# Last chunk of a fused attention and max-out kernel: first-half output products two blocks sooner, second-half token blocks completed one behind the other

## The chip, the cores and the metric

The kernel runs on one core of a Trainium2 chip (trn2). The metric is the device time of one execution in microseconds (us); the profile's span, from the first to the last instruction, is some 2 us shorter. Engines are called PE (TensorE), VectorE (DVE in the profile), ScalarE (ACT), GpSimd (POOL) and SP.

## The reference, cut to what matters

```python
def reference(q, k, v, tau, w1, w2, w3, w_out):       # q, k, v: (4, 6144, 256)
    ...                                               # attention over channels, gives x (24576, 256)
    h = np.maximum(np.maximum(x @ w1, x @ w2), x @ w3)   # (24576, 768)
    return h @ w_out                                     # (24576, 256), float32
```

The attention matrix is multiplied into the three weights ahead, so that for each chunk of 512 tokens the kernel computes three products per block of 128 hidden columns, takes their maximum, and multiplies by w_out. Only the last of 48 chunks is changed.

## The kernel before

The tokens of the last chunk go in two halves of two token blocks (256 columns). `h_block` makes one block of 128 of the 768 hidden columns (fc is 0 to 5): six matmuls on PE, one ScalarE copy, two VectorE maxima, and, where `two_copies` is set, a second ScalarE copy that gives the second maximum two bf16 operands outside PSUM, where the matmuls leave their results (the tiles h_ps and o_ps). The result of a block is called ht; a *product* below is one matmul of ht with w_out. PEld in the views is PE loading the weights of a matmul, here ht itself for a product.

```python
def h_block(gi, aw, fc, tsl=slice(0, TPC), two_copies=False):
    ...
    hp = []
    for m in range(3):
        t = htile(f"h_ps{m}")[:, :n]
        for ic in range(CC):
            PE.matmul(...)                                              # L432
        hp.append(t)
    s_mx = mx_pool.tile([P, CHUNK], BF16, name="s_mx")[:, :n]
    ACT.activation(out=s_mx, in_=hp[0], func=AF.Copy)                   # L436
    DVE.tensor_tensor(out=s_mx, in0=hp[1], in1=s_mx, op=ALU.max)        # L437
    last = hp[2]
    if two_copies:
        last = mx_pool.tile([P, CHUNK], BF16, name="s_h2")[:, :n]
        ACT.activation(out=last, in_=hp[2], func=AF.Copy)               # L441
    DVE.tensor_tensor(out=ht, in0=last, in1=s_mx, op=ALU.max)           # L442

def last_chunk(gi, aw, pending):
    ...
    def products(ps, t0, i, fcs): ...                                   # L504: one matmul for each fc

    def first_half(i):
        if i == 0:
            first["ps"] = xtile("o_ps")
        products(first["ps"], 0, i, range(FC))
        if i == HT - 1:
            ACT.activation(out=o_sb[:, 0:HT, :]..., in_=first["ps"], func=AF.Copy)   # L515
            SP.dma_start(out=dst[:, 0:HT, :], in_=o_sb[:, 0:HT, :])                  # L516

    for fc in range(FC):
        h_block(gi, aw, fc, slice(0, HT))                # first half; the chunk before is finished here too
        ...
    for fc in range(FC):
        h_block(gi, aw, fc, slice(HT, TPC), two_copies=fc in (0, 2, 3))
        if fc >= FC - HT:
            first_half(fc - (FC - HT))
    pss = [htile("o_ps") for _ in range(HT)]
    for fcs in (range(FC - 1), (FC - 1,)):
        for i in range(HT):
            products(pss[i], HT, i, fcs)
    ACT.activation(out=o_sb[:, HT, :], in_=pss[0][:, 0:d_model], func=AF.Copy)       # L531
    DVE.tensor_copy(out=o_sb[:, HT + 1, :], in_=pss[1][:, 0:d_model])                # L532
    ACT.dma_start(out=dst[:, HT, :], in_=o_sb[:, HT, :])                             # L533
    SP.dma_start(out=dst[:, HT + 1, :], in_=o_sb[:, HT + 1, :])                      # L534
...
keep_order(tc)       # every engine executes in the order in which the program is written
```

Because of `keep_order` each engine works in program order, and so an operation that has to wait holds up all that stand behind it on its engine.

## Time and profile before

| | before |
|---|---|
| time, median (lowest to highest) of the first 3 runs | 572.99 us (572.92 to 573.05) |
| span of the profiled run | 571.0 us |
| busy share PE / VectorE / ScalarE | 97% / 74% / 55% |
| granted PE clock | 1.0 |

The views are read from the end backwards: which engine did the last thing, what released it, and what each engine did in the microseconds ahead of that. The lines stand in the prediction, with how each is read. A bracket at the end of a line of a timeline is the idle time of that engine ahead of it, with what ended it; gaps up to 0.15 us get no bracket.

### The profile page before, as it was taken

How to read it: one execution, taken by the hardware profiler on the slowest of the kernel's cores; microseconds unless marked ns; L12 is line 12 of the kernel's file. 1: busy time of each engine (PE TensorE's matmuls, PEld its weight loads, DVE VectorE, ACT ScalarE, POOL GpSimd, SP SyncE). 2: the span in 40 equal slices, each digit the busy share in tenths (PEclk: the TensorE clock that was granted, in tenths of full speed). 3: DMA queues.
4: the chain of work that ended last, by engine and by line, in shares of the span. 5: the costliest groups of instructions: out<-in, count | busy, mean ns of one | idle time of the engine just before them, and what ended most of it. 6: DMA issues, size and time to landing. Idle time of an engine off the chain costs nothing.

```text
span 571.0 us, 9570 instructions
## 1 busy us (share of the span) xinstructions
PE 553.7 (97%) x3395; PEld 328.5 (58%) x3398; DVE 422.9 (74%) x663; ACT 316.4 (55%) x552; POOL 233.4 (41%) x237
## 2 busy tenths in 40 slices
PE   3799999999999999999999999999999999999997
PEld 2665555555755555555575555555575555555566
DVE  0378777877887777777767777777768778778775
ACT  1274567677464576776535467767635444444444
POOL 2442257776450078776560048776750000000000
PEclk9999999999999999999999999999999999999999
DMA  9995999894379169884179359894437333132111
GB/s 144 105 171 111 137 227 132 160 135 115 99 91 178 55 120 155 128 154 100 57 132 151 100 73 144 148 142 100 119 83 157 75 77 108 56 102 65 56 57 74
DMA packets 76960, 65.64 MB, mean 115 GB/s; under 512 B 52464, under 2 KB 62576, under 8 KB 76784
## 3 DMA queue, kind: packets, MB, share of 16 engines
q0 software_dynamic: 19072, 26.48, 38.8%
q1 hardware_dynamic: 57696, 38.41, 24.4%
q8 instruction: 26, 0.43, 0.3%
q14 instruction: 22, 0.18, 0.1%
q10 hardware_dynamic: 144, 0.13, 0.1%
HBM read 78.64 MB, written 25.17 MB: 182 GB/s over the span
## 4 chain that ended last, share of the span: by engine, by line
PE 93%; DMA 5%; POOL 0%; issue 0%; DVE 0%; ACT 0%; ACTq 0%; DVEq 0%; POOLq 0%
PE h_ps L432 65%; PE o_ps L479 22%; DMA q_sb<-in_q_dram 5%; PE gram L285 3%; PE ew_ps L331 3%; POOL k_sb L100 0%; PE o_ps L504 0%; PE h_ps L453 0%; PE ew_ps L359 0%; PE vt_ps L416 0%; DVE aw_sb L368 0%; PE warm_ps L201 0%; DVE o_sb L532 0%; ACT sqa L185 0%; PE rs_ps L353 0%
## 5 line engine op out<-in xcount | busy, mean ns | idle before, releaser
L432 PE MATMUL h_ps<-vt_sb,aw_sb 128*128 128x512 bf16 (+1 forms) x1758 | 404.9, 375 | 0.0
L432 PEld LDWEIGHTS <-aw_sb 128*128 128x128 bf16 x1758 | 171.3, 98 | 160.6 <-DVE aw_sb L337 2.4
L437 DVE TENSOR_TENSOR s_mx<-h_ps,s_mx 128x512 bf16<-128x512 f32 (+1 forms) x293 | 198.2, 676 | 79.2 <-ACT s_mx L436 78.9
L436 ACT ACTIVATE s_mx<-h_ps 128x512 bf16<-128x512 f32 (+1 forms) x293 | 171.7, 586 | 122.5 <-PE h_ps L432 121.2
L442 DVE TENSOR_TENSOR ht_sb<-h_ps,s_mx 128x512 bf16<-128x512 f32 (+1 forms) x290 | 198.3, 684 | 32.7 <-PE h_ps L432 1.9
L244 POOL TENSOR_TENSOR acc<-acc,sq 128x768 f32<-128x768 f32 x88 | 144.3, 1649 | 69.2 <-ACT sq L236 53.1
L479 PE MATMUL o_ps<-wo_sb,ht_sb 128*128 128x256 bf16 x1128 | 153.9, 273 | 0.0
L479 PEld LDWEIGHTS <-ht_sb 128*128 128x128 bf16 x1128 | 110.4, 98 | 52.2 <-DVE ht_sb L442 0.2
L482 ACT ACTIVATE o_sb<-o_ps 128x512 f32<-128x512 f32 x94 | 56.1, 597 | 83.9 <-PE o_ps L479 83.9
L111 POOL DMA_DIRECT2D v_sb<-in_v_dram x48 | 27.7, 582 | 38.7 <-DMA vt_sb<-v_sb 35.2
L236 ACT ACTIVATE sq<-q_sb 128x768 bf16<-128x768 fp8e4 x48 | 40.5, 845 | 0.0
L236 ACT ACTIVATE sq<-k_sb 128x768 bf16<-128x768 fp8e4 x48 | 40.1, 835 | 0.0
L241 POOL CAST acc<-sq 128x768 f32<-128x768 bf16 x6 | 4.9, 820 | 65.4 <-ACT sq L236 65.4
L103 POOL DMA_DIRECT2D q_sb<-in_q_dram x33 | 18.4, 565 | 3.5 <-DMA v_sb<-in_v_dram 3.1
L171 PE MATMUL kk<-k_sb 128*128 128x256 fp8e4 x48 | 7.5, 338 | 11.7 <-DVE k_sb L157 6.2
L100 POOL DMA_DIRECT2D k_sb<-in_k_dram x29 | 16.0, 554 | 3.0 <-DMA v_sb<-in_v_dram 1.1
L185 ACT ACTIVATE sqa<-q_sb 128x1024 bf16<-128x1024 fp8e4 (+2 forms) x9 | 6.8, 768 | 18.1 <-DMA q_sb<-in_q_dram 18.1
L285 PE MATMUL gram<-k_sb,q_sb 128*128 128x512 fp8e4 x144 | 16.8, 276 | 0.0
L334 ACT ACTIVATE aw_sb<-ew_ps,rinv 128x384 bf16<-128x384 f32 (+1 forms) x24 | 13.2, 554 | 5.7 <-PE ew_ps L331 4.8
L285 PEld LDWEIGHTS <-q_sb 128*128 128x256 fp8e4 x144 | 15.9, 136 | 0.6
L257 POOL PARTITION_ALL_REDUCE tot<-acc x6 | 10.9, 1858 | 12.1 <-DVE s_mx L437 6.1
L331 PE MATMUL ew_ps<-w_sb,et 128*128 128x384 bf16 (+1 forms) x96 | 15.8, 313 | 0.0
(73 smaller groups left out, 128.1 us busy)
## 6 DMA issues: line engine op xcount, KB each, us to landing
out_dram<-o_sb SPq DMA_DIRECT2D x41, 512.0 KB, 2.9
v_sb<-in_v_dram POOLq DMA_DIRECT2D x48, 256.0 KB, 4.3
k_sb<-in_k_dram POOLq DMA_DIRECT2D x24, 192.0 KB, 5.9
q_sb<-in_q_dram POOLq DMA_DIRECT2D x24, 192.0 KB, 7.3
out_dram<-o_sb SPq DMA_DIRECT2D x13, 256.0 KB, 2.0
k_sb<-in_k_dram POOLq DMA_DIRECT2D x5, 256.0 KB, 10.6
w_sb<-in_moe_w_dram POOLq DMA_DIRECT2D x9, 128.0 KB, 5.7
kf<-in_k_dram SPq DMA_DIRECT2D x1, 1024.0 KB, 4.7
```

Of the source, the lines that this page charges most:

```text
L103: POOL.dma_start(out=qk[b][0][:, g0:g0 + w, :], in_=q_r[b][:, g0:g0 + w, :])
L111: POOL.dma_start(out=t, in_=v_r[gi // NCH, gi % NCH])
L236: ACT.activation(out=sq, in_=src, func=AF.Square)
L244: POOL.tensor_tensor(out=acc, in0=acc, in1=sq, op=ALU.add)
L285: PE.matmul(g[:, j * C:(j + 1) * C], lhsT=qt[:, tsl, j * P:(j + 1) * P], rhs=kt[:, tsl, :], start=(tp == 0 and j == 0), stop=(tp == NG // ...
L331: PE.matmul(ew[:, :w], lhsT=et[:, j, ic * P:(ic + 1) * P], rhs=w_sb[m][:, j, fsl], start=(j == 0), stop=(j == CC - 1))
L432: PE.matmul(t.rearrange("p (t n) -> p t n", n=P), lhsT=aw[m][:, ic, fsl], rhs=vt[:, tsl, ic, :], start=(ic == 0), stop=(ic == CC - 1))
L436: ACT.activation(out=s_mx, in_=hp[0], func=AF.Copy)
L437: DVE.tensor_tensor(out=s_mx, in0=hp[1], in1=s_mx, op=ALU.max)
L442: DVE.tensor_tensor(out=ht, in0=last, in1=s_mx, op=ALU.max)
L479: PE.matmul(st["ps"][:, half], lhsT=ht[:, fc, t * P:(t + 1) * P], rhs=wo_sb[:, fc, :], start=(fc == 0), stop=(fc == FC - 1))
L482: ACT.activation(out=st["o"][:, t - 1:t + 1, :].rearrange("p t d -> p (t d)"), in_=st["ps"], func=AF.Copy)
```

## The change

Its intent, as far as the code tells it: do the output products of the first half (F0 and F1) after the second half's blocks 2 and 3 instead of 4 and 5, so that their output is copied and stored sooner; complete token block 0 of the second half ahead of block 1, so that its copy and store lie ahead of the other's and not beside it; and give the second ScalarE copy to other blocks.

```diff
--- before.py
+++ after.py
@@ -521,13 +521,13 @@
                 pending[fc - 1]()
         for fc in range(FC):
 
-            h_block(gi, aw, fc, slice(HT, TPC), two_copies=fc in (0, 2, 3))
-            if fc >= FC - HT:
-                first_half(fc - (FC - HT))
+            h_block(gi, aw, fc, slice(HT, TPC), two_copies=fc in (0, 1, 4))
+            if HT <= fc < 2 * HT:
+                first_half(fc - HT)
         pss = [htile("o_ps") for _ in range(HT)]
-        for fcs in (range(FC - 1), (FC - 1,)):
-            for i in range(HT):
-                products(pss[i], HT, i, fcs)
+
+        for i, fcs in ((0, range(FC - 1)), (1, range(2)), (0, (FC - 1,)), (1, range(2, FC))):
+            products(pss[i], HT, i, fcs)
         ACT.activation(out=o_sb[:, HT, :], in_=pss[0][:, 0:d_model], func=AF.Copy)
         DVE.tensor_copy(out=o_sb[:, HT + 1, :], in_=pss[1][:, 0:d_model])
         ACT.dma_start(out=dst[:, HT, :], in_=o_sb[:, HT, :])
```

## The prediction

> **What bounds the kernel now.** I read four views, in this order: the chain that ended last, in order of time; the timelines of PE, VectorE and ScalarE for the last chunk; and the DMA view of the last 5 us. The page says that PE is 97% busy over a span of 571.0 us at full clock, so only the last 12 us, which the change touches, matter here. I call the second-half blocks of the last chunk s0 to s5 (fc 0 to 5), and the two groups of six products of the first half F0 and F1.
>
> The chain, its last pieces (start us, us, what):
>
> ```profile
> 559.91 4.14 PE h_ps L432 x36
> 564.04 0.66 PE o_ps L504 x6
> 564.70 0.66 PE h_ps L432 x6
> 565.36 1.98 PE o_ps L504 x18
> 567.33 0.02 issue
> 567.36 0.42 DVE o_sb L532
> ```
>
> PE sets the end. Six matmuls of 256 columns take 0.66 us (0.109 each) in each of the short pieces. The 36 in the first piece should take 36 x 0.109 = 3.93 and take 4.14: PE waits some 0.2 us there, for PSUM buffers that VectorE has not yet read. The 36 are the last first-half block and s0 to s4; then come F0, s5, F1 and the twelve products of the second half. Behind PE stand the VectorE copy of the last token block (0.42), its store and the closing of the program.
>
> VectorE in the same stretch (start us, us, ...; the bracket is idle time before it):
>
> ```profile
> 560.85 0.42 DVE L437 TENSOR_TENSOR s_mx<-h_ps,s_mx 128x256 bf16<-128x256 f32 x1 [0.63 <-ACT s_mx L436]
> ...
> 564.04 0.42 DVE L437 TENSOR_TENSOR s_mx<-h_ps,s_mx 128x256 bf16<-128x256 f32 x1
> 564.56 0.29 DVE L442 TENSOR_TENSOR ht_sb<-s_h,s_mx 128x256 bf16<-128x256 bf16 x1
> 564.77 0.42 DVE L437 TENSOR_TENSOR s_mx<-h_ps,s_mx 128x256 bf16<-128x256 f32 x1
> 565.29 0.43 DVE L442 TENSOR_TENSOR ht_sb<-h_ps,s_mx 128x256 bf16<-128x256 f32 x1
> 565.63 0.41 DVE L437 TENSOR_TENSOR s_mx<-h_ps,s_mx 128x256 bf16<-128x256 f32 x1
> 566.15 0.43 DVE L442 TENSOR_TENSOR ht_sb<-h_ps,s_mx 128x256 bf16<-128x256 f32 x1
> ```
>
> From 560.85 to 566.58 VectorE has no bracket at all: it is the full engine of the tail, and works off the blocks about 0.6 us behind PE. From start to start: L437 to its L442 0.52; L442 to the next L437 0.34 if it reads PSUM, 0.21 if it reads ScalarE's copy ("two copies"). A block costs 0.86, or 0.73 with two copies, against 0.66 on PE. The last block's result (ht of s5) is there at 566.58; PE asks for it at about 566.83, after F1 and ten products. So there is 0.2 us to spare, and PE, not the latency of s5, sets the end.
>
> ScalarE, with F1's copy to o_sb last but one:
>
> ```profile
> 563.33 0.38 ACT L441 ACTIVATE s_h<-h_ps 128x256 bf16<-128x256 f32 x1
> 563.61 0.38 ACT L436 ACTIVATE s_mx<-h_ps 128x256 bf16<-128x256 f32 x1
> 564.95 0.38 ACT L436 ACTIVATE s_mx<-h_ps 128x256 bf16<-128x256 f32 x1 [0.96 <-PE h_ps L432]
> 566.10 0.60 ACT L515 ACTIVATE o_sb<-o_ps 128x512 f32<-128x512 f32 x1 [0.76 <-PE o_ps L504]
> 567.25 0.38 ACT L531 ACTIVATE o_sb<-o_ps 128x256 f32<-128x256 f32 x1 [0.56 <-PE o_ps L504]
> ```
>
> L515 runs after all six blocks' copies, where it holds up nothing. Back to back, 256-column copies start 0.28 apart (563.33, 563.61); after a 512-column copy the next starts 0.49 later (559.95 to 560.44 in the same timeline). A copy starts 0.31 after the start of the last matmul that it needs (s5: matmul 564.64, copy 564.95).
>
> The stores, 566 to 571 us in 40 slices of 0.125 us, and their landing:
>
> ```profile
> DMA  0000000000004999960029999940200000000000
> out_dram<-o_sb ACTq DMA_DIRECT2D x1, 128.0 KB, 1.9
> out_dram<-o_sb SPq DMA_DIRECT2D x1, 128.0 KB, 2.3
> ```
>
> The store of the first half moves in the first group of nines; the last two, issued 0.15 us apart (567.66 and 567.81 in the timelines), fill the second without a gap. The one issued second takes 2.3 us against 1.9. The span ends 0.9 us after that landing (570.1).
>
> **What the Trainium skill says.** "TensorE: Matmul & The Clock Gate", Part 2, step-by-step: PE pulls weight loads ahead, but matmuls stay in program order. The trace agrees: with a load one matmul ahead, matmuls follow each other every 0.109 us. So a product that waits for ht holds up all products behind it. "VectorE: DVE Perf Modes", the perf-mode tier table: tensor_tensor runs at 2x on 16-bit SBUF operands and 1x with any PSUM operand. The trace agrees in direction, 0.29 against 0.42. "DMA: Bandwidth & Descriptors", Anatomy of one DMA, gives a constant of about 2 us, mostly the write receipt (for the GpSimd path); these SP and ACT stores land after 1.9 to 2.3, of which the strip shows only about 0.45 us of movement for each of the last two. "PSUM — Partial Sum Buffer" bears on the flags of two interleaved groups, but they lie in two banks as before, so nothing follows for time.
>
> **The change part by part.** No instruction is added or removed, on any engine: 12 matmuls move ahead of s3 and s4, the order of the last 12 changes, and three blocks still have two copies, now 0, 1, 4. Everything is in orders and waits.
>
> PE up to s2 is as before; s2's last matmul starts at 562.26. Then, at 0.109 each: F0 562.37, s3 563.02, F1 563.67, s4 564.33, s5 564.98, products from 565.64. The two waits for PSUM in s3 and s4 (0.2 us) go, because F0 gives VectorE time. But s5 begins 0.45 later than before (564.98 against 564.54), since two groups of products (1.31 us) now lie ahead of it instead of one (0.66), less the 0.2.
>
> Between s5 and the first use of its ht only seven products remain (five of token block 0, two of block 1): 7 x 0.109 = 0.76, so PE asks for ht at 566.40. Before, sixteen lay between.
>
> When is it ready? F1's last matmul starts at 564.22, so L515 starts at 564.53 and stands in ScalarE's order ahead of the copies of s4. The first of these would be ready at 564.75 but starts at 564.53 + 0.49 = 565.02 and ends 565.40. Then VectorE: s3 is done at 564.98 (same sums of 0.86 and 0.73, other order), it idles to 565.43; s4 L437 565.43, L442 565.95, s5 L437 + 0.21 = 566.16, L442 + 0.52 = 566.68, end 567.11. (ScalarE's others: s4's second copy 565.30, s5's 565.58 to 565.96, both in time.) The load of the waiting product starts 0.05 after VectorE's end (555.64 to 555.69 at line 479 shows that), its matmul 0.11 later: 567.27. Four products of block 1 follow, the last at 567.27 + 4 x 0.109 = 567.70. Before it was 567.05 (567.36 less 0.31). So PE idles some 0.75 us, and the last VectorE copy is 0.65 later, at 568.01.
>
> In return block 0's copy is at 567.27 + 0.31 = 567.58, its store at about 568.0, block 1's store at 568.01 + 0.45 = 568.46. They are 0.46 apart instead of 0.15, about one movement's length, so the last should land after 2.0 instead of 2.3 us. That is 0.3 back.
>
> Sum: +0.65 on the chain, -0.3 on the landing = +0.35. 572.99 + 0.35 = 573.3.
>
> **The rivals.**
> 1. The order works as meant: s5's ht comes in time, PE loses no time, 0.2 of PSUM waits and 0.3 of store are won: 572.5. Against it: even with an idle ScalarE and VectorE, s5 from 564.98 needs 0.11 + 0.31 (second matmul, latency) + 0.41 (copy, hand-over) + 0.52 + 0.43 + 0.05 + 0.11 = 1.94, so the eighth product is at 566.92 and not at 566.51 and the last matmul at 567.36, 0.3 later than before. With the store's 0.3 that is a draw: 573.0. I count that draw as the real second case: it needs L515 not to delay s4.
> 2. The stores gain nothing: what made the second slower was the queue, not the other store. Then +0.65: 573.6. For it: only one pair is to be seen. Against it: the strip shows the two movements adjoining.
> 3. PSUM buffers go to blocks in another order and s5 waits for one of s4's (565.4). PE loses up to 0.3 there, but it is waiting later anyway; only if s5's first product got it would ht be 0.15 later: 573.5.
>
> **Range and chances.** The draw at 573.0 and the no-gain at 573.6 are on either side of 573.3; repeats agree to 0.13 us (572.92 to 573.05), and a changed program may shift stores by 0.1 to 0.2. So 572.7 to 573.8. Two per cent is 11.5 us, as much as the whole tail: within 2% is all but certain (0.99), faster 0.005, slower 0.005.
>
> **What would show it.** In the changed profile: L515 near 564.5 with s4's copy right behind it; a bracket of about 0.45 on VectorE before s4's L437; a wait of about 0.7 on PE's loads for ht in the last products; the chain passing from PE over VectorE's L442 and ScalarE instead of PE alone; the PSUM waits of s3 and s4 gone; the last two stores about 0.45 apart and the last landing near 2.0 us. I am wrong if PE runs through the products without a wait, if the time is below 572.7, or if the last store still takes 2.3.

## The result

| | before | changed |
|---|---|---|
| median of 4 runs (lowest to highest) | 572.95 us (572.67 to 573.05) | 573.16 us (573.11 to 573.44) |
| ratio | | 1.0005, 95% interval 0.9988 to 1.0023 |
| span of the profiled run | 571.0 us | 571.4 us |

A ratio is the mean time of one kernel's fast runs over that of the other's of the same rounds, so it is not quite the ratio of the two medians. The four runs of each do not overlap, but the interval includes 1: a time within 2% is certain. The medians are 0.21 us apart, less than the 0.33 to 0.38 us over which the runs of one kernel spread, so that the changed kernel is slower at all is suggested and not shown by the times alone. The traces show more, because they can be compared part by part.

For that a common zero is needed. The whole changed run lies 0.07 us later already in front of the changed part: VectorE's first operation with a bracket in the last chunk starts at 560.92 and not at 560.85. So 0.07 is taken off all times of the changed kernel below where the text says "aligned".

The chain that ended last, in order of time, of the changed kernel (start us, us, what):

```profile
559.98 2.62 PE h_ps L432 x24
562.60 0.66 PE o_ps L504 x6
563.25 0.66 PE h_ps L432 x6
563.91 0.67 PE o_ps L504 x6
564.58 0.03 ACTq L515
...
564.65 0.04 ACT o_sb L515
564.69 0.45 issue
565.14 0.14 ACT s_mx L436
...
565.41 0.39 ACT s_h L441
565.80 0.29 ACT s_mx L436
...
566.29 0.43 DVE s_mx L437
...
566.82 0.43 DVE ht_sb L442
...
567.30 0.73 PE o_ps L504 x5
...
568.05 0.43 DVE o_sb L532
```

Before, this chain was PE alone up to the last copy. Now it leaves PE at 564.58, where F1 ends, passes through ScalarE (the copy of the first half's output, L515, then the copies of s4 and s5), then VectorE's maxima of s5, and comes back to PE for five products only. The waits of 0.2 us that stood in the 36 matmuls of before are gone: there the trace has them in s3 and s4, where one matmul comes 0.23 us after the one ahead of it and another 0.20, instead of 0.109. Each starts 0.05 us after VectorE ends an operation that reads PSUM for s1 (562.87 and 563.39), which bears out the reading that PE waited for these buffers. Now s3 takes 0.66 (third line above), and s4 and s5 are one row without a wait:

```profile
564.40 1.47 PE L432 MATMUL h_ps<-vt_sb,aw_sb 128*128 128x256 bf16 x12
```

VectorE and ScalarE in the timeline of the changed kernel:

```profile
564.63 0.42 DVE L442 TENSOR_TENSOR ht_sb<-h_ps,s_mx 128x256 bf16<-128x256 f32 x1
565.55 0.43 DVE L437 TENSOR_TENSOR s_mx<-h_ps,s_mx 128x256 bf16<-128x256 f32 x1 [0.50 <-ACT s_mx L436]
566.08 0.29 DVE L442 TENSOR_TENSOR ht_sb<-s_h,s_mx 128x256 bf16<-128x256 bf16 x1
566.29 0.42 DVE L437 TENSOR_TENSOR s_mx<-h_ps,s_mx 128x256 bf16<-128x256 f32 x1
566.82 0.42 DVE L442 TENSOR_TENSOR ht_sb<-h_ps,s_mx 128x256 bf16<-128x256 f32 x1
```

```profile
564.65 0.60 ACT L515 ACTIVATE o_sb<-o_ps 128x512 f32<-128x512 f32 x1 [0.76 <-PE o_ps L504]
565.14 0.38 ACT L436 ACTIVATE s_mx<-h_ps 128x256 bf16<-128x256 f32 x1
565.41 0.39 ACT L441 ACTIVATE s_h<-h_ps 128x256 bf16<-128x256 f32 x1
565.67 0.41 ACT L436 ACTIVATE s_mx<-h_ps 128x256 bf16<-128x256 f32 x1
```

VectorE, which had no bracket here before, stands still for 0.50 us until s4's copy is there. That copy has no bracket: it follows straight on L515. Its matmul starts at about 564.51 (the second of the block that PE starts at 564.40), and by the 0.31 us that a copy follows on its matmul elsewhere it could have run from 564.82; it started at 565.14, 0.32 later. In the kernel before, L515 ran behind all the blocks' copies. From s4's first maximum on VectorE has no bracket again: s5's L437 starts 0.21 after s4's L442, the usual distance, while its own copy is done 0.21 earlier (565.67 + 0.41). So s5's start on VectorE was set by s4's two maxima ahead of it, which s4's late first copy delayed; the chain view, which infers what released each step, names the copies of s4 and s5 instead.

PE's weight loads for the last twelve products, same timeline:

```profile
565.60 0.42 PEld L504 LDWEIGHTS <-ht_sb 128*128 128x128 bf16 x4
566.43 0.22 PEld L504 LDWEIGHTS <-ht_sb 128*128 128x128 bf16 x3 [0.40 <-DVE ht_sb L442]
567.29 0.44 PEld L504 LDWEIGHTS <-ht_sb 128*128 128x128 bf16 x5 [0.64 <-DVE ht_sb L442]
```

PE's loads wait twice for a result of VectorE: ahead of the fifth product for s4's (0.40), and ahead of the eighth for s5's (0.64). From start to start, these two matmuls come 0.40 and 0.63 after the one ahead instead of 0.109, so PE itself loses 0.29 and 0.52. Before, none of the last 18 loads (F1 and the twelve products) waited:

```profile
565.08 1.95 PEld L504 LDWEIGHTS <-ht_sb 128*128 128x128 bf16 x18
```

The stores of the changed kernel, in the same 40 slices from 566 to 571 us, and their landing:

```profile
DMA  2898992000000000000000059947991000000100
out_dram<-o_sb ACTq DMA_DIRECT2D x1, 128.0 KB, 1.9
out_dram<-o_sb SPq DMA_DIRECT2D x1, 128.0 KB, 1.9
```

The first half's store has already moved in the first slices. The last two, issued at 568.03 and 568.51 (0.48 apart), now show a dip between their two movements, and the second lands in 1.9 us instead of 2.3 (1.91 and 2.25 in the trace). The timelines have the issues, of the changed kernel and then of the kernel before:

```profile
568.03 0.37 ACTq L533 DMA_DIRECT2D out_dram<-o_sb  x1
568.51 0.33 SPq L534 DMA_DIRECT2D out_dram<-o_sb  x1
```

```profile
567.66 0.41 ACTq L533 DMA_DIRECT2D out_dram<-o_sb  x1
567.81 0.33 SPq L534 DMA_DIRECT2D out_dram<-o_sb  x1
```

The account, aligned: the last store is issued 568.51 - 567.81 - 0.07 = 0.63 later, and lands in 0.3 to 0.4 less (1.9 for 2.3, both rounded). That leaves about 0.3. The spans (571.4 and 571.0) differ by 0.4, of which 0.07 lies ahead of the changed part.

The packets of each queue say where the second store lost its time before. Its first packet moved 1.11 us after its issue (568.92), and 0.85 us after it in the changed kernel (569.36); so 0.25 of the 0.34 lies ahead of its first packet. At 0.85 after its issue (568.66) the ScalarE queue's store was moving (568.58 to 569.06), while SP's own earlier store had moved its last data at 568.34. The DMA view of the kernel before for 568.35 to 568.91 has packets of one queue alone, ScalarE's:

```profile
q10 hardware_dynamic: 113, 0.12, 57.7%
```

### The profile page after: what moved, and what is told of

Same layout as the page of the kernel before. It is cut to its first block, busy times and chain, and to the rows that moved or that the text cites. A ratio compares the mean times of both kernels' runs of the same rounds, so it can differ in the third digit from the quotient of the medians.

```text
span 571.4 us, 9570 instructions
## 1 busy us (share of the span) xinstructions
PE 553.3 (97%) x3395; PEld 327.8 (57%) x3398; DVE 423.0 (74%) x663; ACT 316.6 (55%) x552; POOL 233.4 (41%) x237
## 4 chain that ended last, share of the span: by engine, by line
PE 93%; DMA 5%; POOL 0%; issue 0%; DVE 0%; ACT 0%; ACTq 0%; DVEq 0%; POOLq 0%
PE h_ps L432 65%; PE o_ps L479 22%; DMA q_sb<-in_q_dram 5%; PE gram L285 3%; PE ew_ps L331 3%; POOL k_sb L100 0%; PE o_ps L504 0%; PE h_ps L453 0%; PE ew_ps L359 0%; PE vt_ps L416 0%; DVE ht_sb L442 0%; DVE aw_sb L368 0%; PE warm_ps L201 0%; DVE s_mx L437 0%; DVE o_sb L532 0%
## 5 line engine op out<-in xcount | busy, mean ns | idle before, releaser
L437 DVE TENSOR_TENSOR s_mx<-h_ps,s_mx 128x512 bf16<-128x512 f32 (+1 forms) x293 | 198.2, 676 | 80.1 <-ACT s_mx L436 79.9
L442 DVE TENSOR_TENSOR ht_sb<-h_ps,s_mx 128x512 bf16<-128x512 f32 (+1 forms) x290 | 198.3, 684 | 32.7 <-PE h_ps L432 1.9
```

## The experiments

None of them gave a result, and nothing in this document rests on one.

**The new order of the last twelve products alone.** Edit to the kernel before:

```diff
-        for fcs in (range(FC - 1), (FC - 1,)):
-            for i in range(HT):
-                products(pss[i], HT, i, fcs)
+        for i, fcs in ((0, range(FC - 1)), (1, range(2)), (0, (FC - 1,)), (1, range(2, FC))):
+            products(pss[i], HT, i, fcs)
```

> The kernel before with the new order of the last twelve products alone; first-half products and copies stay as they were. Theory (stores collide; the chain is PE, ht of s5 from VectorE at 566.6): the eighth product's load asks at 566.5 and gets ht at 566.63, so PE loses 0.1 us, the last VectorE copy starts 0.1 later (567.5); the last two stores are issued about 0.45 us apart and the last lands in 1.9 instead of 2.3. Sum -0.2 us against before: faster than both. Rival (the new product order is itself what costs the 0.65 us on PE): +0.4 or more and a wait of over 0.5 on PE's loads. Rival (second store is slower for another reason than the first): landing stays 2.3 and the time +0.1.

Measured: nothing. Open with it: whether the gain on the stores is to be had without the loss on PE, in a version better than both.

**The first half's products sooner, with the old order of the last twelve.** Edit to the changed kernel: the diff above the other way round.

> The changed kernel with the old order of the last twelve products (first-half products still two blocks sooner, copies 0, 1, 4). Theory: ht of s5 is still late, at 567.1, because the blocks s4 and s5 come later and ScalarE takes the first half's output copy before s4's; PE waits for it about 0.2 to 0.3 us with only two products behind it, last VectorE copy at 567.7, that is +0.33 against before; stores 0.15 apart again and landing in 2.3; time +0.3 against before, about 0.1 above the changed kernel. Rival (product order made the loss): no wait on PE, time 0 or below against before.

Measured: nothing. Open: how much of the 0.63 us the earlier first half makes by itself.

**The first half's output copy behind the blocks.** Edit to the changed kernel:

```diff
-            if i == HT - 1:
-                ACT.activation(out=o_sb[:, 0:HT, :]..., in_=first["ps"], func=AF.Copy)
-                SP.dma_start(out=dst[:, 0:HT, :], in_=o_sb[:, 0:HT, :])
...
+        ACT.activation(out=o_sb[:, 0:HT, :]..., in_=first["ps"], func=AF.Copy)
+        SP.dma_start(out=dst[:, 0:HT, :], in_=o_sb[:, 0:HT, :])
         pss = [htile("o_ps") for _ in range(HT)]
```

> The changed kernel with the first half's output copy and store issued after the six blocks, so that ScalarE serves s4 and s5 first. Theory (ScalarE's order cost about 0.28 of the delay of ht): s4's copy at 564.8 to 564.9, the bracket before VectorE's s4 operation 0.15 to 0.2 instead of 0.50, ht of s5 at about 566.9 instead of 567.25, last VectorE copy 0.27 sooner than in the changed kernel; time about 0.25 below the changed kernel, so level with before (+0.05). Rival (the delay is only that PE starts s5 later, or PSUM buffers): nothing changes, +0.2 to +0.4 against before.

Measured: nothing. Open: whether the 0.32 us that s4's copy starts late reach the end in full, or whether another wait takes their place. An estimate from the changed kernel's trace: with s4's copy at 564.82, VectorE's operations on s4 and s5 move forward by the same 0.32, s5's L437 to 565.97; s5's copy, which can start 0.28 after s4's second (565.26), would be done at about 565.92. So nothing seen there would take the place of the 0.32.

**The other choice of blocks with two copies alone.** Edit to the kernel before:

```diff
-            h_block(gi, aw, fc, slice(HT, TPC), two_copies=fc in (0, 2, 3))
+            h_block(gi, aw, fc, slice(HT, TPC), two_copies=fc in (0, 1, 4))
```

> The kernel before with the new choice of blocks for the second copy (0, 1, 4 for 0, 2, 3) alone. Theory: VectorE's sum is the same, so ht of s5 comes at 566.6 as before, time within 0.1 us of before; PE's waits for PSUM may move between blocks. Rival (the choice of blocks carries part of the loss): ht of s5 and the time later by 0.2 or more.

Measured: nothing. Open: whether that choice matters at all in the kernel before. In the changed one it should: VectorE stands idle ahead of s4, so time won on earlier blocks is lost there, while s4's second copy shortens the way to ht of s5 by 0.13 (a block of 0.73 for 0.86). That is an estimate from the traces and no run.

## Why the prediction was right

The predicted time was 573.3, the measured median 573.16, inside the range of 572.7 to 573.8. That says little by itself: the range also holds the draw at 573.0, the 573.6 without a gain on the stores, and the time of the kernel before, and 573.16 is as near to the draw as to the forecast. The 0.1 to 0.2 us allowed in it for shifted stores rests on no measurement. What bears the prediction out is that its steps are found in the trace, in its order and nearly in its sizes. What follows compares the two traces; it shows what happened in each, and not what each part of the change would have done alone.

- **PE up to s5.** Predicted: the PSUM waits of 0.2 go and s5 starts at 564.98. Measured: s4 and s5 start at 564.40 as one row of twelve matmuls, so s5 at 564.40 + 6 x 0.109 = 565.05, aligned 564.98. The waits are gone. Right.
- **ScalarE.** Predicted: L515 at 564.53, s4's copy at 565.02. Measured, aligned: 564.58 and 565.07. The term was 0.05 short: L515 starts 0.36 after F1's last matmul and not 0.31. Two waits of ScalarE's own queue stand ahead of it; the second ends at 564.61, 0.04 after the end of that matmul, and L515 starts 0.04 later. The kernel before has the same two waits and the same 0.36 (565.74 to 566.10), so this could have been read beforehand. Right in kind.
- **VectorE.** Predicted: idle for 0.45 ahead of s4, ht of s5 done at 567.11. Measured: 0.50, and 566.82 + 0.42 = 567.24, aligned 567.17. The 0.06 is ScalarE's 0.05 handed on.
- **PE's wait.** Here a step was missing, and a sum was off. The prediction had the seven products ahead of the waiting one run without a break. The fifth of them needs s4's ht, which is done at 566.08 + 0.29 = 566.37, and the load waited 0.40 for it. The prediction's own times had this wait: it has s4's L442 at 565.95, so done at 566.24, and the fifth product due at 566.08. It cost nothing more, because PE waited for s5 afterwards in any case: the eighth product starts at 567.30, aligned 567.23, against 567.27 predicted. The predicted idle time of 0.75 doesn't follow from its own times either (567.27 - 566.40 = 0.87; the 566.51 of its first rival is 566.40 by the same count). Measured: 567.30 - (565.71 + 0.76) = 0.83. The forecast of the end did not use the 0.75.
- **The end of PE's work.** Predicted: last VectorE copy 0.65 later. Measured: 568.05 - 567.36 - 0.07 = 0.62.
- **The stores.** Predicted: 0.46 apart, the last landing in 2.0, 0.3 back. Measured: 0.48 apart, 1.9, 0.3 to 0.4 back. The direction was right and the size a little small. That the other store was the cause is supported by the strips (no gap between the movements before, a dip after) and by the single stores of 256 KB on the same queue, which landed in 2.0 (median of 13) although they are twice as large. The packets fit too: at the time at which it would have begun, only the other store was moving. But both the distance to that store and the distance to SP's own earlier store grew with the change (from 0.15 to 0.48 and from 1.09 to 3.24 between the issues), and no experiment parts them.
- **The sum.** Predicted +0.35; the tails differ by about 0.3, and the medians by 0.21.

Of the rivals, the first (all goes as meant, PE loses nothing) is refuted by the waits of 0.40 and 0.64. Its weaker form, the draw at 573.0, needed L515 not to hold up s4, and the trace shows that it did; the time alone would not have told. The second (no gain on the stores) would have left 2.3 for the landing, and it is 1.9. The third (s5 waits for a PSUM buffer) shows nowhere: its matmuls follow one another without a gap in the row of twelve. What stays open is how the 0.62 divides between the later start of s4 and s5, L515's place in ScalarE's order, and the new order of products. The chain names L515 and what follows it; s5's own matmuls are not on it (565.17 + 0.31 = 565.48, before its copy at 565.67), and it can't name an order of products. By the estimate above about half, 0.32, is L515's place; only taking one away at a time would have shown it, and parted the other two.

## What to carry to other kernels

Work moved forward to fill an early gap of one engine is taken from the place where it hid a later latency: here sixteen products lay between the last block and the first use of its result, and afterwards seven. When a group of products moves forward, its output copy moves along, and on an engine with a fixed order that copy then stands ahead of the copies on which the end depends. Count both before the move, and look at the end of the chain for stores that are issued together: where the last two were issued further apart, the second landed 0.34 us sooner after its issue. That this is to be had without the rest was not tested.

## What the Trainium skill lacked or had wrong

- "TensorE: Matmul & The Clock Gate", Back-to-back issue gap, gives about 131 ns per matmul for a sustained stream of loads and matmuls at 512 columns and says that its isolated figure of 216 ns over-counts. In this kernel it is the isolated figure that holds: in the chain of the kernel before, six matmuls of 512 columns take 1.29 us, 0.215 each, and six of 256 columns 0.66, 0.109 each.

```profile
544.85 1.29 PE h_ps L432 x6
```

- "DMA: Bandwidth & Descriptors", Anatomy of one DMA, has a constant of about 2 us plus the bytes at 436 GB/s for DMAs issued from GpSimd. For stores from SP or ACT these runs show 2.0 for 256 KB and 1.9 for 128 KB as a whole; by the page's rate that leaves 1.4 and 1.6 us (an estimate), so its constant is too large for them. The page has no figure for a store issued just behind another: 2.3 against 1.9 at 0.15 and 0.48 us apart, one pair each.
- No page has the time from a matmul's start to that of the ScalarE copy waiting for it: 0.31 us at 256 columns (0.27 of it the matmul's own duration in the trace), 0.36 where two queue waits stand ahead of the copy.
